# One matrix product from unsplit float32 blocks, behind dummy products, in a hand-ordered three-stage kernel

## The chip, the cores and the metric

The kernel runs on one core of one Trainium2 chip. The metric is device time in microseconds (us) of one execution. A difference of 0.2% or less can't be told from no change.

## What is computed

The reference chains three layers on two batches (b) of 768 positions and 512 channels.

```python
# attention: 8 heads of 64 channels, local window and block summaries
k_sum, v_sum = max and mean of k and v over blocks of 32      # 24 summaries
scores = concat(scale * q k^T where |i-j| < 16, scale * q k_sum^T + log 32)
x = softmax(scores) @ concat(v, v_sum)
# gated layer
gate = sigmoid(causal 5-tap convolution of x, per channel)
x = (gate * (x @ w_val)) @ w_out
# spatial gating
h = relu(x @ w_in);  u, v = halves of h
v_n = (v - mean(v)) / sqrt(var(v) + 1e-6)
out = (u * (w_spatial @ v_n + b_spatial)) @ w_out2
```

There is no nonlinearity between `w_out` and `w_in`, so the kernel forms the product `w_out @ w_in` once ("the weights' product"): 512x512 by 512x1024, and uses it in place of the two.

## The kernel before, in words

**Split products.** Large matrix products are made from a float32 operand split into a high and a low part in the format fp32r: `hi` is the rounded copy (ScalarE, CAST), `lo` is the difference (GpSimd, a tensor_tensor). A product is then three fp32r matmuls (hi·hi, hi·lo, lo·hi), `mm3` and `product`. Scores, transposes, the product with v and the means' matmuls use plain float32 operands.

**Loading weights.** The weights come as float64. `load64` loads a block of 128 rows by 512 numbers (512 KB) and turns it into float32: one ScalarE activation (Prelu) into PSUM, one VectorE tensor_scalar and one VectorE scalar_tensor_tensor. `split64` then makes `hi` and `lo` of it. `w_out` has 4 blocks, each half of `w_in` has 4 (threads `in0`, `in1`), `w_val` 4 and `w_out2` 4.

**The weights' product** (`w_product`) has two halves of 512 columns. For half 1 four PSUM banks collect over the four blocks, in four steps of 4x3 matmuls 128x128 by 512 columns. For half 0 (`OUTER = 1`) each of four steps makes one bank's 4x3 matmuls. ScalarE scales each result into a `wide` tile, which is split again later (`weights_v`, `weights_u`).

**Means of v.** `reduce_v` adds up the rows of v in a tree on VectorE. `put_vsum`, the first time for a batch, brings the 4x24 sums to partitions 96 to 119 by four float32 matmuls with a shifted identity (`moves`), and ScalarE scales them by 1/32 out of PSUM. GpSimd then copies them beside each pair's v (24x1536), which the product with v (`pv`) needs.

**Order.** The work is cut into pieces of named threads (`score`, `at`, `pv`, `wp`, ...). `ORDER` lists the pieces; the place in the list is the priority. `Planner.plan` simulates the engines with a table of costs and gives each engine, and the DMA queue on SP, a fixed order: at each point the operation that can start first, and of those within `LOOK` the one with priority. A PSUM tile may only be taken if it is among the first tiles not yet taken, as many as banks are free (8). SP keeps at most 8 transfers under way.

**SBUF.** 33 units of 128x1536 float32. A small tile is a part of a unit (`Parts`); the parts are dealt out as the program is recorded, and a unit comes free when all its parts are done with.

In the profile all instructions carry line 226, where the planner issues them; the tiles in SBUF units are all called at_u and those in PSUM at_ps.

Of the kernel before, what the change touches and what calls it, by code (L numbers as in the profile page):

```python
# [16 lines left out]
P = 128  # L17
# [19 lines left out]

SEVEN = {'val': (), 'u': (), 'v': ()}
# [4 lines left out]
    wout wval in0 in1 lk wout wp in1 wout lk kw wp wval kw in1 lk in0 lq wp wout lk mask lq in1 in0 kw lq*2 mask lv  # L43
    score wp in0 vsum score kw vsum lk wp score cw lv*2 lq put*2 score*2 wval at put lv put wp*2 lk at wval pv at
    score*2 wp pv at score lv lq at pv*2 gate val0 lk pv val0 at lv val0 at val0 lk wu at lv kw wu score wu pv kw wu
    wv at lq kw pv*2 score wv kw wv u0 vsum u0 gate wv score val0 vsum val0 u0 lv put*2 score*2 pv at lq val0 u0
    score*2 pv score at v0 put v0 put val0 at*3 pv*4 at pv at pv ws v0*2 gate val1 f0 val1 gate v0*2 val1*3 u1 val1
    out2 val1 ws s0 v1 u1 val1 v1*2 u1 f1 s1 f0 u1 ws v1*3 f1 s0 s1 f0 f1 u0 u1 s1*2 ws u1 s0*2 ws f1 u0 u1 u0 u1
    out2 f0 s0 out2 s0 u0 s1 s0*2 f0 s0 s1 out2 s0 ws f0*2 s0 s1 ws s1 s0 r s0*2 f1 r s1*2 r f1 s1 r*3 f1 s1*2 r*3
    s1 r*3  # L50
# [12 lines left out]
class Planner:  # L63
# [6 lines left out]
    def __init__(self, nc):  # L70
        self.ops, self.hist, self.tiles, self.cap = [], {}, {}, {}
        self.seq = 0
        self.piece, self.needs = [("start", 0)], {}
        self.homes, self.place = {}, {}
# [3 lines left out]
    def tile(self, ap, tag, bufs):  # L78

        name = ap.tensor.name if hasattr(ap, "tensor") else ap.name  # L80
        self.tiles[name] = [tag, None, 0]
        self.cap[tag] = bufs
        return ap
# [126 lines left out]
    def issue(self):  # L210
        order, real_ = self.plan(), {}

        def home(x):

            if not hasattr(x, "ap") or x.tensor.name not in self.place:
                return x
            name = x.tensor.name
            if name not in real_:
                tag, i = self.place[name]
                real_[name] = self.homes[tag](i, x.tensor)  # L220
            y = bass.AP(real_[name].tensor, x.offset, list(x.ap))
            return y if y.dtype == x.dtype else y.bitcast(x.dtype)

        for o in order:
            real, method, args, kw = o.call
            getattr(real, method)(*[home(x) for x in args], **{k: home(x) for k, x in kw.items()})  # L226

    def plan(self):
# [17 lines left out]
        held = {}  # L246
        open_, best, stale = {e: [] for e in free}, {e: None for e in free}, set(free)
# [8 lines left out]
        def slot_time(o):  # L256
            want = {}
            for n in o.tiles:
                if n in user:
                    want.setdefault(self.tiles[n][0], []).append(n)  # L260
            t = 0.0
            for tag, names in want.items():
                have = slots[tag]
# [33 lines left out]
        while len(order) < len(ops):  # L297
# [9 lines left out]
            if o.want:  # L307
                for n in sorted(o.tiles):
                    if n in user:
                        tag = self.tiles[n][0]  # L310
                        line[tag].remove(n)
                        held[n] = min(slots[tag])[1]
                        slots[tag].remove(min(slots[tag]))
                        if tag in self.homes:
                            self.place[n] = tag, held[n]
# [33 lines left out]
            for n in o.tiles:  # L349
                uses[n] -= 1  # L350
                if not uses[n]:
                    slots[self.tiles[n][0]].append((done + lat, held[n]))
                    stale.update(free)
# [7 lines left out]
        return order  # L361

# [10 lines left out]
def tile_kernel(ctx, tc, q, k, v, vn, w_val, conv_w, w_out, w_in, w_sp, b_sp, w_out2, mask_l, mask_r, eye, out):  # L373
# [19 lines left out]
    plan.homes["u"] = lambda i, x: homes.tile([P, 1536], x.dtype, tag=f"h{i}", name="at_" + x.name, bufs=1)  # L393

    def unit(dt=F32R):
        uid[0] += 1
        x = homes.tile([P, 1536], dt, tag="h0", name=f"u{uid[0]}", bufs=1)
        return plan.tile(x, "u", NU)

    class Parts:  # L400


        def __init__(self, n, dt=F32R):
            self.n, self.dt, self.free = n, dt, []

        def get(self):
            if not self.free:
                u = unit(self.dt)
                self.free = [u[:, self.n * i : self.n * (i + 1)] for i in reversed(range(1536 // self.n))]
            return self.free.pop()  # L410
# [45 lines left out]
    def load_masks():  # L456

# [15 lines left out]
        pool.memset(moves, 0.0)  # L473
        pool.affine_select(out=moves, in_=moves, pattern=[[-1, 264]], compare_op=ALU.not_equal, fill=1.0, base=112, channel_multiplier=1)
        yield

    def load64(src, n=512, queue=None):

        u = unit(F32)
        raw, t = u[:, : 2 * n], u[:, 2 * n : 3 * n]  # L480
# [12 lines left out]
    W = {}  # L493

    def split64(name, src, c):
        third = Parts(512)
        for i in range(KT):
            t = load64(src[i * P : (i + 1) * P, 1024 * c : 1024 * (c + 1)])
# [4 lines left out]
            yield  # L503

# [56 lines left out]
    def reduce_v(m):  # L561
# [13 lines left out]
        dve.tensor_add(MS[b][:, m % 2 * D : (m % 2 + 1) * D], t[:, :D], t[:, D : 2 * D])  # L575

    def put_vsum(n):
# [4 lines left out]
        need("mask", 2)  # L582
# [12 lines left out]
    def scores(t):  # L595
        n, g = ticks[t]
        need("mask", 1)
# [29 lines left out]
    def a_T(t):  # L627
        need("score", t + 1)
        need("mask", 2)
# [478 lines left out]

    def w_product():
# [5 lines left out]
        for n in (1, 0):  # L1115
            if n < OUTER:
                for e in range(KT):
                    po = psum()
                    for i in range(KT):
                        need("wout", i + 1)  # L1120
                        need(f"in{n}", i + 1)
                        mm3(po, [t[:, e * P : (e + 1) * P] for t in W["ot", i, 0]], W["in", i, n], i == 0, i == KT - 1)
# [4 lines left out]
            for i in range(KT):  # L1127
                need("wout", i + 1)
                need(f"in{n}", i + 1)
                for k, (a, b) in enumerate(((0, 0), (0, 1), (1, 0))):  # L1130
# [12 lines left out]
    def each(n, piece):  # L1143
# [6 lines left out]
        "lk": each(NPR, load_k), "lq": each(NPR, load_q), "mask": load_masks(), "kw": each(NPR, windows), "lv": each(NPR, load_v),  # L1150
# [3 lines left out]
        "wp": w_product(), "wv": each(KT, weights_v), "wu": each(KT, weights_u), "vs": each(2, weights_x), "us": each(2, weights_s), "nw": each(2, weights_n),  # L1154
# [120 lines left out]
```

## Time and profile before

| | |
|---|---|
| median of 3 runs | 271.32 us (271.19 to 271.7) |
| profiled execution, its own time | 271.58 us |
| its span, first to last instruction | 269.8 us |
| TensorE busy | 250.0 us, from 13.44 to 266.8 us |
| mean granted clock | 0.994 |

The profiled execution spends 1.78 us outside its span, and lies 0.26 us above the median. "Busy" counts the time from the start of an instruction to its end; the ends of matmuls are modelled. PE is TensorE, PEld its weight loads, DVE VectorE, ACT ScalarE, POOL GpSimd, SP the engine whose queue issues the loads.

### The profile page before, as it was taken

To read this page: it belongs to the slowest core of one execution; us is meant where nothing else is said; L and a number is where in the kernel's file an instruction comes from. 1 tells how busy PE (TensorE), PEld (TensorE's weight loads), DVE (VectorE), ACT (ScalarE), POOL (GpSimd) and SP (SyncE) were. 2 spreads that over 40 slices of the span, in tenths; PEclk is the share of its full clock that TensorE was granted. 3 is DMA by queue.
4 is the path that set the end of the run, shared out by engine and by line. 5 is a ranking of instruction groups with operands and counts; after the bars stand their busy time and mean duration, and the time that the engine had idled before them with its cause. 6 is when DMAs were issued, how large, how long until landed. Compare 5 with 4: busy or idle time off the path is not lost.

```text
span 269.8 us, 5493 instructions
## 1 busy us (share of the span) xinstructions
PE 250.0 (93%) x1912; PEld 224.8 (83%) x1912; DVE 190.0 (70%) x558; ACT 166.0 (62%) x452; POOL 180.4 (67%) x209
## 2 busy tenths in 40 slices
PE   0097999999999998999999999999999999999995
PEld 0075777868999996988899989899999999989885
DVE  3598888889989998899975969597452924572110
ACT  4687898899999999797353054512465755132221
POOL 7698864797898984993067167652869798883210
PEclk9999899999999999999999999999999999999999
DMA  6999998981452410460000010000003202022213
GB/s 208 405 406 406 312 359 271 325 297 35 137 167 61 117 32 1 129 226 1 2 1 0 10 70 0 0 2 0 0 4 137 97 0 80 0 78 78 80 39 117
DMA packets 11003, 31.63 MB, mean 117 GB/s; under 512 B 1552, under 2 KB 1824, under 8 KB 10976
## 3 DMA queue, kind: packets, MB, share of 16 engines
q1 hardware_dynamic: 10944, 31.27, 33.1%
q8 instruction: 15, 0.25, 0.4%
q14 instruction: 12, 0.10, 0.1%
q0 software_dynamic: 32, 0.02, 0.0%
HBM read 28.14 MB, written 3.15 MB: 116 GB/s over the span
## 4 chain that ended last, share of the span: by engine, by line
PE 79%; DMA 7%; DVE 5%; ACT 4%; SPq 2%; POOL 1%; issue 1%; DVEq 0%; ACTq 0%
PE at_ps L226 79%; DVE at_u L226 4%; DMA at_u<-in_k_dram 4%; ACT at_u L226 4%; DMA at_u<-in_moe_w_val_dram 2%; SPq L226 2%; DMA at_u<-in_v_dram 1%; POOL at_u L226 1%; DVE km L226 0%; ACT at_ps L226 0%; DVE nm L226 0%; DVE sm L226 0%; ACT xl L226 0%; DVEq L226 0%; ACTq L226 0%
## 5 line engine op out<-in xcount | busy, mean ns | idle before, releaser
L226 PE MATMUL at_ps<-at_u,at_u 128*128 128x384 f32 (+4 forms) x1800 | 239.1, 321 | 15.5 <-ACT at_u L226 15.5
L226 PEld LDWEIGHTS at_ps<-at_u,at_u 128*128 128x128 f32 (+2 forms) x1800 | 212.7, 188 | 38.7 <-ACT at_u L226 16.6
L226 POOL TENSOR_TENSOR at_u<-at_u,at_u 128x384 fp32r<-128x384 f32 (+2 forms) x95 | 116.9, 1251 | 48.9 <-ACT at_u L226 47.7
L226 ACT CAST at_u<-at_u 128x384 fp32r<-128x384 f32 (+2 forms) x95 | 53.4, 597 | 29.2 <-DVE at_u L226 19.8
L226 ACT COPY at_u<-at_ps 120x384 f32<-120x384 f32 (+3 forms) x61 | 28.4, 504 | 47.2 <-PE at_ps L226 47.2
L226 DVE TENSOR_TENSOR at_u<-at_ps,at_u 128x384 f32<-128x384 f32 (+1 forms) x36 | 19.7, 553 | 35.2 <-PE at_ps L226 33.8
L226 ACT ACTIVATE at_u<-at_u,nm 128x120 f32<-128x120 f32 x96 | 37.1, 401 | 1.6 <-DVE nm L226 1.6
L226 DVE SCALAR_TENSOR_TENSOR at_u<-at_ps,cw,at_u 128x384 f32<-128x384 f32 (+3 forms) x64 | 37.0, 608 | 0.2
L226 POOL TENSOR_TENSOR at_u<-at_u,sm 128x360 f32<-128x360 f32 x32 | 27.5, 882 | 13.3 <-DVE sm L226 11.2
L226 DVE CUSTOM_DVE_ANT_0 at_u<-at_ps,mask 128x120 f32<-128x120 f32 x96 | 21.6, 276 | 4.4 <-PE at_ps L226 4.3
L226 DVE TENSOR_SCALAR at_u<-at_u 128x512 uint32<-128x512 uint32 (+1 forms) x21 | 15.3, 731 | 6.8 <-DMA at_u<-in_moe_w_out_dram 5.3
L226 ACT ACTIVATION_READ_ACCUMULATOR at_u<-at_u,nm 128x1 f32 x96 | 19.7, 205 | 0.0
L226 ACT ACTIVATE at_ps<-at_u 128x512 f32<-128x512 f32 x20 | 12.9, 643 | 10.7 <-DMA at_u<-in_moe_w_out_dram 6.9
L226 POOL COPY at_u<-at_u 128x320 f32<-128x320 f32 (+2 forms) x24 | 17.8, 756 | 0.8 <-ACT at_u L226 0.2
L226 POOL TENSOR_TENSOR va<-va,power 128x1 f32<-128x1 f32 x12 | 7.4, 618 | 14.9 <-DVE va L226 8.8
L226 DVE TENSOR_TENSOR at_u<-at_u 128x384 f32<-128x384 f32 (+5 forms) x31 | 15.9, 515 | 0.1
L226 ACT ACTIVATE at_u<-at_ps 128x512 f32<-128x512 f32 (+1 forms) x22 | 12.6, 593 | 5.0 <-PE at_ps L226 4.9
L226 DVE TENSOR_TENSOR at_u<-at_u,at_u 128x256 f32<-128x256 f32 (+2 forms) x25 | 15.5, 628 | 0.1
L226 DVE SCALAR_TENSOR_TENSOR at_u<-at_ps,at_u 128x512 uint32<-128x512 uint32 x20 | 13.7, 689 | 2.1 <-ACT at_ps L226 0.8
L226 PE MATMUL at_ps<-moves,at_u 128*120 128x128 f32 x96 | 13.8, 276 | 0.4 <-POOL at_u L226 0.4
L226 DVE SCALAR_TENSOR_TENSOR at_u<-at_u,at_u 128x384 f32<-128x384 f32 x16 | 14.0, 905 | 0.1
L226 PEld LDWEIGHTS at_ps<-moves,at_u 128*120 128x120 f32 x96 | 10.9, 137 | 1.8 <-POOL at_u L226 0.6
(36 smaller groups left out, 116.4 us busy)
## 6 DMA issues: line engine op xcount, KB each, us to landing
at_u<-in_moe_w_out_dram SPq DMA_DIRECT2D x8, 512.0 KB, 5.0
at_u<-in_moe_w_in_dram SPq DMA_DIRECT2D x8, 512.0 KB, 9.0
at_u<-in_k_dram SPq DMA_DIRECT2D x8, 384.0 KB, 8.5
at_u<-in_q_dram SPq DMA_DIRECT2D x8, 384.0 KB, 8.1
at_u<-in_v_dram SPq DMA_DIRECT2D x16, 192.0 KB, 6.0
at_u<-in_vn_dram SPq DMA_DIRECT2D x6, 512.0 KB, 8.5
out_dram<-at_u SPq DMA_DIRECT2D x11, 256.0 KB, 2.0
at_u<-in_moe_w_spatial_dram SPq DMA_DIRECT2D x6, 384.0 KB, 5.8
```

Source lines behind the costliest of these rows:

```text
L226: getattr(real, method)(*[home(x) for x in args], **{k: home(x) for k, x in kw.items()})
```

## The change

1. `WHOLE = {0: 4, 1: 4}`: for all four blocks of both halves, the weights' product takes the unsplit float32 blocks, 32 float32 matmuls of 128x128 by 512 columns in place of 96 fp32r ones. The 12 blocks of `w_out` and `w_in` are no longer split; each lies in a `wide` tile. (`split_late` has no pieces with these values.)
2. A new thread `hot` of nine pieces (`awake`): each multiplies `moves` (128x264) by its first 128 columns into a PSUM tile that nobody reads. `load_masks` makes `moves` first, and the masks after it.
3. The means of v: ScalarE scales the sums (96x128) in place, and four DMAs from the SP queue move them, 24x128 each, to partitions 96 to 119. The four matmuls and the scaling out of PSUM are gone.
4. The planner places parts of units itself (`Units`): a part is taken when its first operation is planned and comes free on its own; parts of one kind share a unit.
5. `ORDER` is another list. `mask`, `in1`, `hot` and `wout` come first, the first four `wp` pieces are spread among the loads and the first scores, and the first `gate` stands again behind eight `score` and four `pv` pieces.

```diff
+WHOLE = {0: 4, 1: 4}
...
-    wout wval in0 in1 lk wout wp in1 wout lk kw wp wval kw in1 lk in0 lq wp wout lk mask lq in1 in0 kw lq*2 mask lv
-    score wp in0 vsum score kw vsum lk wp score cw lv*2 lq put*2 score*2 wval at put lv put wp*2 lk at wval pv at
...
+    mask in1 hot mask hot wout*2 in1 hot*4 in1 wval wout in1 lk lq hot wval wout lk wp lk wp hot lk kw*2 in0*2 score
+    wp lq*2 in0 score kw vsum wp lq in0 vsum score kw score lv score wp*2 at put cw pv lv put score wp at pv lv
+    wval*2 put at score*2 wp lv*2 at lk put hot lk at vsum lv at*2 pv*2 kw gate lq lv lq kw wu lq pv*2 val0 wu
...
+            whole = i < WHOLE[max(c, name == "ot")] and name in ("ot", "in")
+            t = load64(src[i * P : (i + 1) * P, 1024 * c : 1024 * (c + 1)], to=wide.get() if whole else None)
+            if whole:
+                T[name, i, c] = t
+                yield
+                continue
...
+    def awake(i):
+        need("mask", 1)
+        pe.matmul(psum()[:, :264], moves[:, :P], moves, start=True, stop=True)
...
+        if m % 2:
+            act.mul(MS[b], MS[b], 1.0 / 32)
...
         if b not in MEAN:
-            po = psum()
+            MEAN[b] = stage.get()[WK:KW]
             for i in range(4):
-                pe.matmul(po[:KW, i * 2 * D : (i + 1) * 2 * D], moves[: 4 * NS, 16 + i * NS : 16 + i * NS + KW], MS[b], start=True, stop=True, skip_group_check=True)
-            MEAN[b] = stage.get()[WK:KW]
-            act.mul(MEAN[b], po[WK:KW], 1.0 / 32)
+                sp.dma_start(MEAN[b][:, i * 2 * D : (i + 1) * 2 * D], MS[b][i * NS : (i + 1) * NS])
...
+                        if i < WHOLE[n]:
+                            pe.matmul(po, T["ot", i, 0][:, e * P : (e + 1) * P], T["in", i, n], start=i == 0, stop=i == KT - 1)
+                            continue
...
+                if i < WHOLE[n]:
+                    for e in range(KT):
+                        pe.matmul(pos[e], T["ot", i, 0][:, e * P : (e + 1) * P], T["in", i, n], start=i == 0, stop=i == KT - 1)
...
+class Units:
+    def take(self, kind):
+        t, i, j = self.pick(kind)
+        if None not in self.free[i]:
+            self.kind[i], self.free[i] = kind, [t] * (self.WIDTH // kind[1])
+            self.count += 1
+            self.names[i] = self.count
+        self.free[i][j] = None
+        return i, j
+    def give(self, at, t):
+        self.free[at[0]][at[1]] = t
```

## Rows read from the trace of the kernel before

**Rows 1.** The page: span and busy time of each engine, with the count of instructions.

```profile
span 269.8 us, 5493 instructions
PE 250.0 (93%) x1912; PEld 224.8 (83%) x1912; DVE 190.0 (70%) x558; ACT 166.0 (62%) x452; POOL 180.4 (67%) x209
```

**Rows 2.** Busy us of each engine by stretch, granted clock, DMA share, GB/s.

```profile
core 0: us, PE busy (x) PEld busy (x) DVE busy (x) ACT busy (x) POOL busy (x), PEclk, DMA share, GB/s
0.00:13.44 13.44, 0.00 (x0) 0.00 (x0) 6.03 (x10) 7.54 (x12) 9.35 (x26) 1.00 0.83 306
13.44:19.00 5.56, 5.56 (x13) 4.36 (x14) 5.11 (x8) 4.58 (x8) 5.09 (x8) 1.00 1.03 407
22.86:24.21 1.35, 0.00 (x0) 0.00 (x0) 1.25 (x3) 0.99 (x3) 0.41 (x1) 1.00 1.04 410
25.95:29.30 3.35, 3.35 (x15) 2.46 (x13) 2.80 (x10) 2.88 (x12) 3.35 (x8) 0.50 1.06 345
29.30:61.12 31.82, 30.73 (x317) 24.08 (x315) 27.14 (x116) 28.37 (x105) 23.16 (x26) 1.00 0.93 308
72.78:104.23 31.45, 30.51 (x386) 28.15 (x385) 29.14 (x133) 31.36 (x118) 25.59 (x33) 1.00 0.30 93
104.23:266.80 162.57, 162.55 (x1025) 150.38 (x1025) 101.49 (x241) 74.13 (x157) 99.27 (x90) 1.00 0.13 47
266.80:269.80 3.00, 0.00 (x0) 0.00 (x0) 0.00 (x0) 0.37 (x1) 0.00 (x0) 1.00 0.20 69
0.00:72.78 72.78, 56.90 (x503) 46.25 (x504) 59.33 (x188) 60.14 (x179) 55.59 (x87) 0.98 0.82 288
```

**Rows 3.** Timeline of the start: start, duration, engine, operation.

```profile
1.51 0.40 POOL L226 TENSOR_SCALAR_AFFINE_SELECT moves<-moves 128x264 f32<-128x264 f32 x1
4.16 0.66 ACT L226 ACTIVATE at_ps<-at_u 128x512 f32<-128x512 f32 x1 [2.14 <-DMA at_u<-in_moe_w_out_dram]
4.16 0.43 DVE L226 TENSOR_SCALAR at_u<-at_u 128x512 uint32<-128x512 uint32 x1 [4.16 <-DMA at_u<-in_moe_w_out_dram]
6.18 0.69 DVE L226 SCALAR_TENSOR_TENSOR at_u<-at_ps,at_u 128x512 uint32<-128x512 uint32 x1 [0.24 <-ACT at_ps L226]
13.44 9.42 PE L226 MATMUL at_ps<-at_u,at_u 128*128 128x512 f32 x36 [13.44 <-ACT at_u L226]
```

**Rows 4.** TensorE by shape, 13 to 62 us: calls, busy us, mean ns, idle before.

```profile
L226 PE MATMUL at_ps<-at_u,at_u 128*128 128x512 f32 x96 | 28.8, 453 | 14.8 <-ACT at_u L226 14.8
```

**Rows 5.** The same view, 200 to 266.8 us.

```profile
L226 PE MATMUL at_ps<-at_u,at_u 128*128 128x512 f32 x132 | 31.8, 391 | 0.0
L226 PE MATMUL at_ps<-at_u,at_u 128*128 128x256 f32 x24 | 3.0, 283 | 0.0
```

**Rows 6.** Timeline of TensorE and its weight loads at 104 us.

```profile
104.23 1.10 PE L226 MATMUL at_ps<-at_u,moves 96*120 96x128 f32 x8 [0.95 <-DVE at_u L226]
104.20 0.94 PEld L226 LDWEIGHTS at_ps<-at_u,moves 96*120 96x120 f32 x8 [1.34 <-issue]
```

**Rows 7.** TensorE by shape, 13 to 29.3 us.

```profile
L226 PE MATMUL at_ps<-at_u,at_u 64*64 64x120 f32 x24 | 2.4, 334 | 0.0
```

**Rows 8.** All groups by shape: calls, busy us, mean ns, idle before.

```profile
L226 POOL TENSOR_TENSOR at_u<-at_u,at_u 128x512 fp32r<-128x512 f32 x28 | 36.3, 1299 | 8.5 <-ACT at_u L226 7.6 <-DMA at_u<-in_v_dram 0.8
L226 ACT CAST at_u<-at_u 128x512 fp32r<-128x512 f32 x28 | 17.5, 625 | 2.5 <-DVE at_u L226 2.5
L226 PE MATMUL at_ps<-at_u,at_u 64*64 64x120 f32 x384 | 19.0, 309 | 0.0
```

**Rows 9.** VectorE by shape, 0 to 61 us.

```profile
L226 DVE TENSOR_SCALAR at_u<-at_u 128x512 uint32<-128x512 uint32 x16 | 12.9, 813 | 5.7 <-DMA at_u<-in_moe_w_out_dram 4.2 <-DMA at_u<-in_moe_w_in_dram 1.5
```

**Rows 10.** ScalarE's timeline: the first gate.

```profile
72.78 1.53 ACT L226 ACTIVATE at_u<-at_u 128x1536 f32<-128x1536 f32 x1
```

**Rows 11.** DMA issues: queue, count, KB each, median us to landing.

```profile
at_u<-in_v_dram SPq DMA_DIRECT2D x16, 92.0 KB, 4.2
```

**Rows 12.** What SP's queue waited for: us, times, longest.

```profile
SPq L226 <- ACT at_u L226: 56.1, 14, 15.9
```

More of the change, by code (lines that the diff above doesn't have):

```diff
@@ L217, in home @@
             name = x.tensor.name
[L218 to L221, printed above, removed]
+            tag, i, at, key = self.place[name]
+            if key not in real_:
+                real_[key] = self.homes[tag](i, x.tensor)
+            y = bass.AP(real_[key].tensor, x.offset + at, list(x.ap))
             return y if y.dtype == x.dtype else y.bitcast(x.dtype)
@@ L262, in slot_time @@
             for tag, names in want.items():
+                if tag == "u":
+                    reach, left = space.room(), len(names)
+                    for n in line[tag]:
+                        if not reach(self.kind[n]):
+                            return None
+                        left -= n in names
+                        if not left:
+                            break
+                    t = max(t, max(space.pick(self.kind[n])[0] for n in names))
+                    continue
                 have = slots[tag]
@@ L351, in plan @@
                 if not uses[n]:
-                    slots[self.tiles[n][0]].append((done + lat, held[n]))
+                    if self.tiles[n][0] == "u":
+                        space.give(held[n], done + lat)
+                    else:
+                        slots[self.tiles[n][0]].append((done + lat, held[n]))
                     stale.update(free)
@@ L361, in plan, with __init__, room, reach @@
         return order
+class Units:
+    WIDTH = 1536
+    def __init__(self, n):
+        self.kind, self.free = [None] * n, [[0.0] for i in range(n)]
+        self.names, self.count = [0] * n, 0
+    def room(self):
+        whole = sum(None not in x for x in self.free)
+        parts = {}
+        for k, x in zip(self.kind, self.free):
+            if None in x:
+                parts[k] = parts.get(k, 0) + len(x) - x.count(None)
+        def reach(kind):
+            nonlocal whole
+            if parts.get(kind, 0):
+                parts[kind] -= 1
+            elif whole:
+                whole -= 1
+                parts[kind] = self.WIDTH // kind[1] - 1
+            else:
+                return False
+            return True
+        return reach
+    def pick(self, kind):
+        some = [(-x.count(None), i) for i, x in enumerate(self.free) if self.kind[i] == kind and None in x and x.count(None) < len(x)]
+        if some:
+            i = min(some)[1]
+            t, j = min((t, j) for j, t in enumerate(self.free[i]) if t is not None)
+            return t, i, j
+        t, i = min((max(x), i) for i, x in enumerate(self.free) if None not in x)
+        return t, i, 0
+    def take(self, kind):
[8 more added lines that the diff above has]
+        self.free[at[0]][at[1]] = t
 class Recorder:
@@ L393, in tile_kernel, with unit @@
     plan.homes["u"] = lambda i, x: homes.tile([P, 1536], x.dtype, tag=f"h{i}", name="at_" + x.name, bufs=1)
-    def unit(dt=F32R):
+    kinds = [0]
+    def unit(dt=F32R, n=1536, kind=0):
         uid[0] += 1
         x = homes.tile([P, 1536], dt, tag="h0", name=f"u{uid[0]}", bufs=1)
-        return plan.tile(x, "u", NU)
+        return plan.tile(x, "u", NU, (kind, n))[:, :n]
     class Parts:
         def __init__(self, n, dt=F32R):
-            self.n, self.dt, self.free = n, dt, []
+            kinds[0] += 1
+            self.n, self.dt, self.kind = n, dt, kinds[0]
         def get(self):
[L407 to L410, printed above, removed]
+            return unit(self.dt, self.n, self.kind)
     def f(ap):
@@ L491, in load64 @@
         return t
-    W = {}
+    W, T = {}, {}
     def split64(name, src, c):
@@ L596, in scores @@
         n, g = ticks[t]
-        need("mask", 1)
+        need("mask", 2)
         need("lq", n + 1)
@@ L628, in a_T @@
         need("score", t + 1)
-        need("mask", 2)
+        need("mask", 1)
         for h in range(2):
@@ L1107, in weights_u, with split_late @@
         W["p", e, 0] = halves(W32.pop((0, e)))
+    def split_late(i):
+        need("wout", i + 1)
+        if i >= WHOLE[0]:
+            W["ot", i, 0] = halves(T["ot", i, 0])
     def w_product():
```

52 lines of the change are left out of this document (31 added, 21 removed).

## The prediction

> **What bounds the kernel now.** I read the page first: TensorE is busy for 250.0 of 269.8 us, no other engine for more than 190 [rows 1]. Then the busy time by stretch, to see where TensorE is not busy [rows 2]. It starts at 13.44, stands still from 22.86 to 24.21 (1.35 us), for 31.82 - 30.73 = 1.09 between 29.30 and 61.12, for 31.45 - 30.51 = 0.94 between 72.78 and 104.23, and then has no idle time until 266.80; 3.0 us follow for the last result. So the span is 13.44 + 250.0 + 3.4 of gaps + 3.0. A change counts if it moves the start, the sum of TensorE's work, or a gap. Third, the start in the timeline [rows 3]: the first block is there at 4.16, the second is float32 at 6.18 + 0.69 = 6.87, yet the first matmul waits for ScalarE and GpSimd, which split the blocks, until 13.44.
>
> The clock counts too. From 13.44 to 19.00, 13 matmuls of 512 columns take 5.56 us, 428 ns each, which is 512 columns at 1.2 GHz; the column for the granted clock reads 1.00 there, and I go by the durations. (The Trainium skill, "TensorE: Matmul & The Clock Gate", Seeing it yourself, warns that the clock records can be unreliable; by the record there would be no slow start to save.) After the stop at 22.86 the record does fall, to 0.50 from 25.95 to 29.30 [rows 2].
>
> VectorE is the second bound: until 72.78 it is busy 59.33 us [rows 2]. A TensorE that runs ahead will meet it.
>
> **The change part by part.**
>
> *The weights' product.* Before, its 96 matmuls cost 28.8 us [rows 4]; at the full clock such a matmul takes 31.8 / 132 = 0.241 us [rows 5]. After, there are 32 plain float32 matmuls of the same size, which the trace does not show. The nearest rows are the means' matmuls: four of 128 columns are eight records, in 1.10 us [rows 6], so one product is two records of 137 ns. The line through fp32r matmuls of 256 columns (3.0 / 24 = 125 ns) and of 512 (241 ns) is 9 ns + 0.453 ns a column [rows 5]; at twice the slope a record of 128 columns comes to 125 ns, near the 137. With that slope, 512 columns take 2 x (9 + 0.906 x 512) = 946 ns, and 32 of them 30.3 us: 1.5 more than before. Bounds: two records at the fp32r pace, 32 x 2 x 0.241 = 15.4, and all 1.10 / 4 growing with the columns, 32 x 1.10 = 35.2. I take 30.3, since the 137 ns speak against the lower end and include fixed time.
>
> A rule of the Trainium skill speaks against this edit: "FP8 and Floating Point Precision", TensorE Precision Notes, gives true float32 four passes through the array, against the three fp32r matmuls. By it the product would be 32 x 4 x 0.241 = 30.8, the term 2.0 in place of 1.5. The 137 ns for two passes of 128 columns agree.
>
> *Start and dummies.* `moves` was ready at 1.51 + 0.40 = 1.91 behind part of the masks [rows 3]; made first, I put it at 1.7. A dummy of 264 columns costs 264 / 128 x 0.275 = 0.57 at the full clock, 1.13 at half. Before, the clock took from 13.44 to 19.00, 5.56 us, to rise. So five dummies run slowly to 7.3 and the next ones fast. Two of the nine stand in the list behind PSUM tiles of the first `wp` pieces and run late; seven end at about 8.4. The data of the first product is there at 6.9, on the old landings. I take a start at 8.2: -5.2. Bounds: 6.9 (-6.5), and all nine first, 9.5 (-3.9). The late two add 2 x 0.55 = 1.1.
>
> *Scores at the low clock.* The 24 score records up to 29.3 us cost 2.4 [rows 7], the mean of all 384 is 19.0 / 384 = 0.049 [rows 8]: 24 x 0.049 = 1.2, so -1.2 if the clock stays up. Bounds -1.2 and 0.
>
> *The splits.* Twelve CASTs of 0.625 us on ScalarE (7.5) and twelve differences of 1.30 on GpSimd (15.6) go [rows 8]. They are off the path except at the start, already counted. They also lay beside VectorE: its tensor_scalar on a block takes 0.43 alone [rows 3] and 0.81 on average up to 61 us [rows 9]. For 12 blocks that is up to 12 x 0.38 = 4.6 us of VectorE.
>
> *The feed.* What is late next is the first gate, at 72.78 [rows 10]. By then TensorE had worked 56.90 [rows 2]; after the change 56.9 + 1.5 - 1.2 - 1.1 (a mean's matmuls) = 56.1, so it would get there at 8.2 + 56.1 = 64.3. VectorE, at 59.3 - 4.6 of work and the same 13.4 of idle time, gets there at 68.2. So TensorE must find some 4 us of other work or stop. The new list has other products ready (half 0 from 23 us on, the later scores), and the parts of SBUF that come free singly let loads start earlier, so I put all gaps at 3.0, against 3.4: -0.4. Bounds: none (-3.4) and 9 (+5.6).
>
> *The means.* Their eight matmuls go, twice 1.10: -2.2 [rows 6]. The gap of 0.95 before the second set, which waited for VectorE, is among the gaps. In their place ScalarE's scaling and four transfers: about 0.3 us, and some 4 until they land (a transfer of 92 KB takes 4.2 [rows 11]; four of 12 KB should need no more), against 1.10 and 0.59 for the scaling. The copies on GpSimd and `pv` of the batch start 2.6 us later. Scores and products cover that; if they didn't, TensorE would lose 2.6 a batch, within the gaps' bound. On SP the transfers wait for ScalarE, and the loads of k, q and v behind them wait too; SP's queue waited 56.1 us for ScalarE before without starving TensorE [rows 12].
>
> *The placing of parts* issues no instruction of its own. Reuse is finer, so a load may wait for another part than before; the gaps' bounds hold it.
>
> The sum: -5.2 + 1.5 + 1.1 - 1.2 - 0.4 - 2.2 = -6.4. The span goes from 269.8 to 263.4, the execution, with its 1.78 outside the span, to 265.2. The profiled execution lay 0.26 above the median, so the median comes to **264.9** against 271.32.
>
> **The rivals.**
>
> *TensorE is fed throughout.* No gaps after the start, and the product at the array's pace: the gaps give 3.0 more and the product perhaps 1: 260.9. For it: the gaps were only 2.0 after 24.21. Against: VectorE's 68.2 above.
>
> *VectorE keeps its pace.* GpSimd, rid of the splits, does its other work in the same places, tensor_scalars stay slow, and the first gate stays at 72.78. Then only what comes behind it is saved: 1.10 of means and 0.94 of gap, less a late dummy of 0.57: 271.32 - 1.5 = 269.8. For it: VectorE is busy 27.14 of 31.82 and 29.14 of 31.45 around it [rows 2]. Against: 13.4 us of idle time before the gate, half of it in the first 13.44 us.
>
> *No change.* The weight loads of plain float32 are not hidden behind a matmul. The means' loads took 0.94 for eight, 0.117 each [rows 6]; 64 of them uncovered cost 7.5, which turns 264.9 into 272.4, and with 55 uncovered the change does nothing (271.3). Against: in those rows 0.94 of loads lie inside 1.10 of matmuls.
>
> *Slower.* TensorE runs ahead and stops again and again between 23 and 64 us, and the clock falls after each stop. The stop of 1.35 us was followed by 3.35 at half rate [rows 2], together 1.35 + 1.68 = 3.0 lost. The sum holds 3.0 of gaps. So from the point where stops cost 9.4 the gain is gone, a little over three of this size; four give 264.9 + 12.1 - 3.0 = 274.0. For it: the load-bound stretch, DMA share 0.93 and more [rows 2]. Against: there was one such stop in all.
>
> **How the numbers follow.** Forecast 0.60 (262.5 to 267.5), fed throughout 0.13, VectorE's pace 0.11, no change 0.05, slower 0.11. So faster by over 0.2% (what a measurement here can tell) 0.60 + 0.13 + 0.11 = 0.84, within it 0.05, slower 0.11. The range has to take in the second and third case, with the product's and the start's bounds: 260.0 to 270.0.
>
> **What would show it.** Right: in the timeline TensorE's dummies from about 1.7 and its first 512-column product at 7 to 9; 64 records of 512 columns in about 30 us; no CAST and no difference of 128x512 in the first 25 us; tensor_scalars nearer 0.43; the first gate between 64 and 69; no gap at the second means. Wrong: products over 1.05 us each, gaps of TensorE over 6 us between 20 and 70 or a granted clock of 0.5 there more than once, a gate still at 72, or a TensorE that waits for `pv`'s v behind the means' transfers.

## The result, and the profile after

The changed kernel takes 269.01 us (median of four runs, 268.58 to 269.44) against 271.51 for the kernel before beside it: 0.9904 of it, 95% interval 0.9876 to 0.9932. It is faster, as forecast, but by 2.5 us where 6.4 were forecast. The rows are of an execution of 269.44 us.

The page, first the span, then the busy time of each engine; it answers to [rows 1]:

```profile
span 267.7 us, 5433 instructions
PE 255.7 (96%) x1882; PEld 220.7 (82%) x1882; DVE 189.3 (71%) x558; ACT 158.1 (59%) x440; POOL 164.1 (61%) x197
```

Busy us by stretch, as in [rows 2]:

```profile
0.00:8.25 8.25, 5.46 (x15) 4.06 (x15) 2.39 (x5) 2.83 (x4) 4.44 (x21) 1.00 0.74 245
8.25:30.00 21.75, 20.68 (x132) 11.19 (x133) 17.66 (x57) 15.89 (x38) 9.69 (x23) 1.00 1.03 406
30.00:45.00 15.00, 14.42 (x85) 7.71 (x84) 14.21 (x70) 13.67 (x64) 7.25 (x11) 1.00 0.93 280
45.00:60.00 15.00, 11.10 (x129) 7.64 (x128) 8.82 (x33) 11.78 (x42) 9.67 (x11) 1.00 0.77 248
...
60.00:65.00 5.00, 5.00 (x102) 4.76 (x100) 4.96 (x14) 4.75 (x13) 2.02 (x2) 0.66 1.06 247
...
8.25:264.65 256.40, 250.23 (x1868) 216.64 (x1868) 186.94 (x554) 154.89 (x436) 159.64 (x176) 0.99 0.34 115
```

TensorE's timeline to 75 us, those of its rows that begin behind a stop (the bracket: how long it stood, and what ended that); it answers to the start in [rows 3]:

```profile
8.25 1.95 PE L230 MATMUL at_ps<-at_u 128*128 128x512 f32 x4 [0.92 <-DVE at_u L230]
11.28 1.12 PE L230 MATMUL at_ps<-at_u,at_u 128*128 128x512 f32 x2 [1.07 <-DVE at_u L230]
32.77 3.98 PE L230 MATMUL at_ps<-at_u,at_u 64*64 64x120 f32 x30 [0.58 <-DMA at_u<-in_q_dram]
47.09 1.88 PE L230 MATMUL at_ps<-at_u,at_u 64*64 64x120 f32 x44 [0.90 <-ACT at_u L230]
49.61 3.70 PE L230 MATMUL at_ps<-at_u,at_u 128*128 128x512 f32 x8 [0.63 <-ACT at_u L230]
53.50 0.99 PE L230 MATMUL at_ps<-at_u,at_u 120*64 120x64 f32 x24 [0.19 <-POOL at_u L230]
59.28 1.20 PE L230 MATMUL at_ps<-moves,at_u 128*120 128x128 f32 x9 [2.18 <-DVE at_u L230]
```

The account that the prediction opened for the kernel before closes here as 8.25 of start + 250.23 of work + 6.17 of stops (256.40 - 250.23) + 3.05 behind the last product = 267.7. Against before: start -5.2, work +0.2, stops +2.8, end the same: -2.1. Nearly all the stops lie ahead of 59.28 us; from 45 to 60 TensorE works 11.10 of 15 us. From 60 to 65 the granted clock is 0.66. From 8.25 to 30 us the DMA engines are busy throughout (share 1.03, 406 GB/s), as they were from 13.44 us before the change [rows 2]; from 45 to 60, where TensorE stands most, their share is 0.77. So the start came at the forecast's figure, and over half of it was given back within 51 us.

What holds TensorE there is told by ScalarE's timeline and by the chain of waits that ends at 59.28 (start, us, what):

```profile
45.90 0.63 ACT L230 ACTIVATE at_ps<-at_u 128x512 f32<-128x512 f32 x1 [1.56 <-DMA at_u<-in_moe_w_val_dram]
```

```profile
39.82 1.99 ACT at_u L230 x7
41.80 6.63 DMA at_u<-in_moe_w_val_dram
48.44 0.02 issue
48.45 0.77 SPq L230
...
52.70 4.15 DMA at_u<-in_k_dram
56.85 0.02 issue
56.88 0.96 DVE km L230
...
59.24 0.04 issue
59.28 0.76 PE at_ps L230 x5
```

A load of `w_val` lands late, and ScalarE stands 1.56 us in front of its conversion; TensorE's stop of 0.90 before 47.09 is ended by ScalarE. On SP's queue the rest comes later still: the means' transfers, then k of the second batch, which TensorE needs through VectorE. SP's own timeline, one row for a run of transfers of one kind, which includes waits inside the run:

```profile
26.89 14.18 SPq L230 DMA_DIRECT2D at_u<-in_v_dram  x12
41.17 1.81 SPq L230 DMA_DIRECT2D at_u<-in_moe_w_val_dram  x2
43.03 3.70 SPq L230 DMA_DIRECT2D at_u<-in_v_dram  x6
46.82 3.91 SPq L230 DMA_DIRECT2D at_u<-at_u  x4
50.84 1.19 SPq L230 DMA_DIRECT2D at_u<-in_v_dram  x2
52.07 1.05 SPq L230 DMA_DIRECT2D at_u<-in_k_dram  x2
```

The four transfers of the means, 12 KB each, take 3.91 us of the queue. The second goes out at 48.45, when a load of `w_val` that was issued at 41.80 has landed (41.80 + 6.63 = 48.43): this program issues a transfer only when the one eight places ahead of it has landed, whatever their sizes.

### The profile page after: what moved, and what is told of

The parts are those of the page before. It is cut to its first block, busy times and chain, and to the rows that moved or that the text cites. A ratio compares the mean times of both kernels' runs of the same rounds, so it can differ in the third digit from the quotient of the medians.

```text
span 267.7 us, 5433 instructions
## 1 busy us (share of the span) xinstructions
PE 255.7 (96%) x1882; PEld 220.7 (82%) x1882; DVE 189.3 (71%) x558; ACT 158.1 (59%) x440; POOL 164.1 (61%) x197
## 2 busy tenths in 40 slices
DMA packets 11291, 31.73 MB, mean 119 GB/s; under 512 B 1648, under 2 KB 2112, under 8 KB 11264
## 4 chain that ended last, share of the span: by engine, by line
PE 73%; DMA 17%; SPq 3%; POOL 3%; ACT 2%; DVE 1%; issue 1%; DVEq 0%; ACTq 0%
PE at_ps L230 73%; DMA at_u<-in_moe_w_out_dram 6%; DMA at_u<-in_k_dram 5%; DMA at_u<-in_q_dram 4%; SPq L230 3%; POOL at_u L230 3%; DMA at_u<-in_moe_w_val_dram 2%; ACT at_u L230 2%; DVE at_u L230 0%; DVE km L230 0%; ACT at_ps L230 0%; DVEq L230 0%; ACTq L230 0%
## 5 line engine op out<-in xcount | busy, mean ns | idle before, releaser
L230 PE MATMUL at_ps<-at_u,at_u 128*128 128x384 f32 (+4 forms) x1752 | 233.5, 323 | 4.0 <-ACT at_u L230 2.1
L230 PEld LDWEIGHTS at_ps<-at_u,at_u 128*128 128x128 f32 (+2 forms) x1752 | 202.4, 190 | 31.6 <-issue 11.6
L230 POOL TENSOR_TENSOR at_u<-at_u,at_u 128x384 fp32r<-128x384 f32 (+2 forms) x83 | 102.8, 1261 | 53.1 <-ACT at_u L230 50.9
L230 ACT CAST at_u<-at_u 128x384 fp32r<-128x384 f32 (+2 forms) x83 | 45.3, 589 | 32.1 <-DVE at_u L230 26.7
L230 POOL TENSOR_TENSOR at_u<-at_u,sm 128x360 f32<-128x360 f32 x32 | 25.1, 814 | 18.9 <-ACT at_u L230 9.5
L230 DVE SCALAR_TENSOR_TENSOR at_u<-at_ps,cw,at_u 128x384 f32<-128x384 f32 (+4 forms) x64 | 36.3, 610 | 0.0
L230 ACT ACTIVATE at_ps<-at_u 128x512 f32<-128x512 f32 x20 | 13.0, 652 | 20.7 <-DMA at_u<-in_moe_w_out_dram 11.4
L230 DVE TENSOR_TENSOR at_u<-at_u,at_u 128x256 f32<-128x256 f32 (+2 forms) x25 | 19.8, 793 | 1.3 <-PE at_ps L230 0.7
L230 ACT ACTIVATE at_u<-at_ps 128x512 f32<-128x512 f32 x20 | 11.6, 596 | 14.2 <-PE at_ps L230 14.1
L230 DVE TENSOR_SCALAR at_u<-at_u 128x512 uint32<-128x512 uint32 (+1 forms) x21 | 11.5, 547 | 9.3 <-DMA at_u<-in_moe_w_in_dram 5.6
L230 DVE BATCH_NORM_STATS2 st<-at_u 128x6 f32<-128x512 f32 x12 | 8.2, 688 | 7.3 <-ACT at_u L230 7.3
```

## Experiments

Times vary by chip, so each kernel is given as its ratio to the kernel before on the same chip, with the 95% interval; 0.001 is 0.27 us, and the changed kernel stands at 0.9904. "Plan kept" means that the order is that of the changed kernel, and the edit sits in `issue`, where the planned operations are handed out (line numbers in the rows shift with it). The theories named in the expectations: S, the start and the unsplit product are worth what they were priced at; F, engines that work in order stand in front of single late loads, so the order of the loads matters; V, VectorE's work sets the pace; L, the transfers bind as a sum, eight under way at most, so that a load moved ahead makes another late.

**Without dummies.**

```diff
+            if o.piece[0] == "hot":
+                continue
```

> The changed kernel with its planned order kept, less the nine dummy products. Theory S (the start is worth what it was priced at): the first product still starts near 8.2 us, but at 1.2 GHz for some 5.6 us, which loses 2.8 us; the time goes from 269.0 to 271 or more. Theory F (TensorE waits for loads that SP's queue issues late, 6 us of gaps between 10 and 60 us): most of the 2.8 us goes into waiting that is there anyway; the time stays within 268.5 to 270. Theory V (VectorE's work sets the pace until the first gate at 71.2): the gate moves by less than 0.5 us and so does the end.

0.9892 (0.9853 to 0.993): the same as with them. Its first products run at half the rate:

```profile
8.14 3.78 PE L232 MATMUL at_ps<-at_u 128*128 128x512 f32 x4 [8.14 <-DVE at_u L232]
...
45.00:60.00 15.00, 11.56 (x129) 8.21 (x128) 8.79 (x35) 12.71 (x44) 10.82 (x12) 0.92 0.79 240
```

Four records take 3.78 us where 1.95 were needed behind the dummies. But they fill the stop of 1.07 at 10.2, so the third pair of records is only 1.1 us behind (13.35 for 12.24), and the late dummies' 1.3 us are saved. The dummies are worth nothing here. S had said 271 or more and is in doubt, but 1.1 us is too little to settle what an early start is worth; the late start below does that.

**The means' transfers from ScalarE's queue, and GpSimd's zeroing of v's tiles early; then both.** The zeroing (`memset`) is put as early as its tile is free.

```diff
+            if method == "dma_start" and o.piece[0] == "put":
+                real = self.ACT.real
...
+            if o.call[1] == "memset" and o.piece[0] == "lv":
+                done.insert(i, o)
```

> The changed kernel with its planned order kept; only the eight transfers of the means are issued from ScalarE's queue in place of SP's. Theory F: SP no longer spends 3.9 us on the first four, the loads of k for batch 1 are issued near 48 us in place of 52.1, the copies of the means on GpSimd start near 46 to 48 in place of 52.0, VectorE's wait of 4.3 us for k shrinks, and the time falls to 265.5 to 267.5. Theory V: the loads move, but the first gate stays within 0.5 us of 71.2 and the time at 268.5 to 269.5. Theory S says nothing changes, since neither the start nor the product does.

> The changed kernel with its planned order kept, but GpSimd's zeroing of each v tile, for which SP's loads of v wait, is put as early on GpSimd's queue as its SBUF unit allows. Theory F: SP is released sooner between 30 and 46 us, the loads behind come 0.5 to 3 us earlier, time 267 to 268.5. Theory V: first gate and time unchanged within 0.5 us. If the 8 transfers under way are what holds SP, and not GpSimd, nothing changes either.

> Both edits of the two runs before: means from ScalarE's queue and early zeroing. Theory F: the effects add, time 264.5 to 267, first gate at 66 to 69. Theory V: time 268.5 to 269.5, first gate within 0.5 us of 71.2.

ScalarE's queue: 1.0006 (0.9987 to 1.0025), the whole gain lost. Early zeroing: 0.9883 (0.9847 to 0.992), no difference that can be told. Both: 1.0003 (0.9978 to 1.0028). The first shows TensorE at 6.61 us of work from 40 to 50 in place of 8.47, and ScalarE here:

```profile
48.20 0.66 ACT L232 ACTIVATE at_ps<-at_u 128x512 f32<-128x512 f32 x1 [4.43 <-DMA at_u<-in_moe_w_val_dram]
...
44.97 0.82 SPq L232 DMA_DIRECT2D at_u<-in_moe_w_val_dram  x2
```

The loads of `w_val` left SP at 44.97 in place of 41.17, and ScalarE stood 4.43 us. So freeing SP of the means this way made the loads later, not earlier; neither F nor V had this. The chain of waits shows why SP fell behind (start, us, what):

```profile
42.67 2.23 DMA at_u<-at_u
...
44.97 3.21 DMA at_u<-in_moe_w_val_dram
...
48.21 3.86 DMA at_u<-at_u
```

ScalarE, behind its other work, issues the first transfer of the means at 42.67; it lands at 44.90, and only then does SP issue the load of `w_val`, for which ScalarE then stands until 48.20 before it can issue the next transfer of the means. In this program the eight places are one count over both queues: the means left SP's queue, but kept their places, and SP stood 3.2 us for one of them. So the run is no test of F.

**k of the second batch ahead of v's third pair,** without and with early zeroing.

```diff
+            if o.piece[0] == "lk" and o.piece[1] in (4, 5) and o.call[1] == "dma_start":
+                done.insert(i, o)      # i: behind v's second pair on SP's queue
```

> The changed kernel with its planned order kept on every engine; only the two loads of k for batch 1 that SP issues at 52.1 us, behind the means' transfers, are put ahead of the loads of v's third pair, near 33 us. Theory F (late loads stop the in-order engines, and TensorE behind them): VectorE's wait of 4.3 us at 50.8 goes, TensorE's gap of 2.2 us at 57 goes with it and the clock stays up after it, time 265.5 to 267.5. Theory L (the transfers are bound by their sum: what is loaded earlier pushes the v and w_val loads back by 2 us): gaps move to 45 to 55 us, time 268.5 to 270.

> The edit of the run before together with the early zeroing of v's tiles. Theory F: 265 to 267. Theory L: 268 to 270.

0.9903 (0.9867 to 0.9939) and 0.9885 (0.9857 to 0.9913): no gain. In the first the stop of 2.18 us in front of the transposes is gone, and another has come:

```profile
49.08 7.91 PE L230 MATMUL at_ps<-at_u,at_u 64*64 64x120 f32 x76 [2.73 <-ACT at_u L230]
```

That speaks for L: k came earlier, `w_val` later (at 42.02 on SP in place of 41.17).

**The means by matmuls again, and the product from split blocks again;** both planned anew with the new list (in the second `WHOLE = {0: 0, 1: 0}`).

```diff
-                sp.dma_start(MEAN[b][:, i * 2 * D : (i + 1) * 2 * D], MS[b][i * NS : (i + 1) * NS])
+                pe.matmul(po[:KW, i * 2 * D : (i + 1) * 2 * D], moves[: 4 * NS, 16 + i * NS : 16 + i * NS + KW], MS[b], start=True, stop=True, skip_group_check=True)
...
-WHOLE = {0: 4, 1: 4}
+WHOLE = {0: 0, 1: 0}
```

> The changed kernel with the means moved by matmuls again as before the change; the planner makes a new order from the same list. TensorE gets 2.2 us of work back. Theory F (the transfers of the means lie in SP's way and land late): put starts 5 us earlier and TensorE's gaps between 45 and 60 us shrink by more than 2.2, time at or below 269. Theory L: gaps as they are, time 270.5 to 272.

> The changed kernel with the weights' product from split blocks again (96 fp32r matmuls, 12 CASTs and 12 differences back), dummies, means, parts and list as changed; the planner makes a new order. TensorE's work falls by 30.6 - 23 to 28, that is 3 to 7 us, ScalarE gets 7.5 and GpSimd 15.6 us back. If the unsplit product is what the change gains by: first product near 12 us, more gaps, time 271 to 276. If the gain is in the list and the start alone: 266 to 270.

1.0046 (1.0 to 1.0092) and 1.0471 (1.0428 to 1.0513). The split product starts nearly as early and then stops again and again, for ScalarE and GpSimd:

```profile
8.83 0.50 PE L230 MATMUL at_ps<-at_u,at_u 128*128 128x512 f32 x1 [0.80 <-ACT at_u L230]
9.65 0.49 PE L230 MATMUL at_ps<-at_u,at_u 128*128 128x512 f32 x1 [0.32 <-POOL at_u L230]
10.88 6.88 PE L230 MATMUL at_ps<-at_u,at_u 128*128 128x512 f32 x22 [0.74 <-POOL at_u L230]
```

The first is at or above the upper end of what L had said, the second beyond both expectations. The list was not made for these two, so they don't price the parts; they show that the new list is no gain without the parts that it was made for.

**What does the work on SP's queue cost?** First the means' transfers left out; second v's two large transfers of a pair issued as one.

```diff
+            if o.piece[0] == "put" and method == "dma_start":
+                continue
...
+            if o.piece[0] == "lv" and method == "dma_start" and args[0].ap[0][1] == 64:
+                d, s = args
+                if d.offset % 1536:
+                    continue
+                args = [bass.AP(x.tensor, x.offset, [list(x.ap[0]), [1, 1536]]) for x in args]
```

> Plan kept; the eight transfers of the means are left out, and GpSimd's copies read a constant instead of the means of v, so the block means do not enter the product. ScalarE still scales the sums. Theory L (the transfers, eight under way at most, are late as a whole): SP is free of 3.9 us of issuing and of four places among the eight, the loads of k for the second batch are issued at about 48 instead of 52.07, TensorE's stop of 2.18 us before 59.28 shrinks below 1, idle time of TensorE between 45 and 60 falls from 3.9 to 2 or less, time 267. Theory V (VectorE's work sets the pace): the date of the first gate and the time stay within 0.5 us of 269.0.

> Plan kept; the two large transfers of each pair's v, 64 partitions each, are issued as one of twice the bytes, so 32 transfers of v become 24. Theory L, if the count of transfers under way matters: v's first three pairs are issued 1.5 to 3 us sooner, what follows them on SP's queue too (the load that TensorE waits for before 47 us, the means', k), idle time between 45 and 60 falls below 3, time 267.5 or less. L, if only the bytes matter: no change, 269.0 within 0.5. V: no change either.

0.9794 (0.9769 to 0.9819) and 0.9844 (0.9817 to 0.987): 3.0 and 1.6 us less than the changed kernel. Without the means' transfers (SP, TensorE from 45 to 60, the first gate):

```profile
49.74 0.96 SPq L240 DMA_DIRECT2D at_u<-in_k_dram  x2
...
45.00:60.00 15.00, 13.16 (x156) 9.11 (x155) 9.78 (x36) 12.66 (x44) 10.34 (x12) 0.89 0.95 277
...
68.58 1.50 ACT L240 ACTIVATE at_u<-at_u 128x1536 f32<-128x1536 f32 x1
```

Merged v (SP):

```profile
27.03 12.34 SPq L235 DMA_DIRECT2D at_u<-in_v_dram  x9
```

Without the means' transfers k leaves SP at 49.74 in place of 52.07, TensorE stands 1.84 us of the 15 shown in place of 3.90, and the first gate comes at 68.58 (before: [rows 10]; after: 71.19). VectorE's work is the same (189.2 us against 189.3), so V falls. The run also frees GpSimd's copies from waiting for the means, so it does not tell the place on the queue from the lateness of the means. Merging v moves no byte less, and SP's run of v's first three pairs shrinks from 14.18 to 12.34 us: fewer, larger transfers of the same bytes get through sooner. Whether it is the count of transfers or the size of their packets (10651 in place of 11291 in all), the run does not tell. The Trainium skill, "SBUF — State Buffer", The DMA setup-cost knee, says that each transfer pays a part that does not grow with its bytes, and asks for the largest single transfers; here the traces agree: with the means on ScalarE's queue 12 KB took 2.23 and 3.86 us to land, and v's 192 KB took 4.5 in the median.

**The list and the placing of parts,** each put back to that of the kernel before, planned anew.

```diff
-    mask in1 hot mask hot wout*2 in1 hot*4 in1 wval wout in1 lk lq hot wval wout lk wp lk wp hot lk kw*2 in0*2 score
+    mask hot*7 wout wval in0 in1 lk wout wp in1 wout lk kw wp wval kw in1 lk in0 lq wp wout lk mask lq in1 in0 kw lq*2 mask lv
...
-            return unit(self.dt, self.n, self.kind)
+            if not self.free:
+                u = unit(self.dt)
+                self.free = [u[:, self.n * i : self.n * (i + 1)] for i in reversed(range(1536 // self.n))]
+            return self.free.pop()
```

> All of the change but its list: the list of the kernel before, with the first mask piece and seven dummies put in front (the other two dummies fall to the end of the list), planned anew. If the new list is what makes the loads late (more of v's and w_val's early), the gaps of TensorE after its start come back to 3.4 to 4.5, and the time is 265 to 267. If the start is simply absorbed because the loads' sum, not their order, sets the date by which TensorE is fed, the first gate again comes at 70 to 73 and the time is 268 to 272.

> All of the change but the placing of parts: parts are dealt out of whole units as the program is recorded, as in the kernel before, and the plan is made anew with the new list. If the finer placing lets loads start sooner, loads come later here and the time is 1 to 4 us longer (270 to 273). If it is neutral: 269.0 within 0.8. If its finer reuse is what makes loads wait for a neighbour, the gaps between 45 and 60 shrink and the time is 266 to 268.

The old list: 1.0301 (1.0264 to 1.0338). With it the first product starts at 13.88 us all the same, 6.24 us after the dummies, released by VectorE: the two blocks that it needs first are the first and the fourth that the old list loads. Neither expectation was met; the new list is a necessary part of the early start. The old placing: 0.9888 (0.9865 to 0.991), no difference.

**All that helped together.** Left out means' transfers, merged v, early zeroing; then the last two alone, with the whole computation; then these with k ahead of the means on SP's queue; and merged v in the kernel before.

```diff
+            if o.piece[0] == "lk" and o.piece[1] in (4, 5) and o.call[1] == "dma_start":
+                done.insert(i, o)      # i: ahead of the means' transfers on SP's queue
```

> Plan kept; three edits together: v's large transfers issued as one per pair, GpSimd's zeroing of v's tiles early, and the means' eight transfers left out (GpSimd's copies read a constant, so the block means do not enter the product). Theory L, and the three are separate costs on SP's queue: their single gains add up, about 3.0 + 1.6 + 0.6 = 5.2 us, time 264, first gate near 66, and nearly the whole of the forecast comes back. L, but all three relieve one and the same wait: no more than the means' transfers alone, 266 to 267. A limit behind the loads (VectorE, ScalarE): 266 or more, with TensorE's remaining stops released by these engines while SP's queue is ahead.

> Plan kept, whole computation: v's large transfers issued as one per pair, and the zeroing of v's tiles early. L with separate costs: 269.0 - 1.6 - 0.6, about 266.8, faster than the changed kernel. L with one wait: 267.5, as with the merged transfers alone.

> As the run with merged transfers and early zeroing, and on SP's queue the two loads of k for the second batch are issued ahead of the four transfers of the means. If what the means' transfers cost is the delay of k behind them (some 4 us on SP's queue), TensorE's stop before its transposes at 57 to 59 us goes and the time falls by another 1 to 2 us, to 265.5. If they cost through the places they hold among the eight under way, or the means are now late for the product with v, no gain: 266.8 or more, with a stop of TensorE released by GpSimd in its place.

> The kernel before, plan kept, with v's large transfers issued as one per pair. If transfers bound the front only since the change (before, TensorE's gaps between 29 and 61 us were 1.09), no more than 0.5 us: 271.0. If they bound it before as well, the same 1.6 us as in the changed kernel: 269.8.

0.978 (0.9735 to 0.9824), 0.9806 (0.9771 to 0.984), 0.9802 (0.9765 to 0.9838) and 1.0021 (0.9996 to 1.0045). The three do not add up: on top of the other two, leaving out the means' transfers gives 0.0026, inside the intervals, where alone it gave 0.0110. That they relieve one and the same wait is the nearest reading; that engines behind the loads set the rest is not excluded. Merged v with early zeroing keeps the whole computation and is faster than both kernels, 267.55 us beside 272.0 in the median (the quotient of these medians, 0.984, is the upper end of the interval). What the early zeroing adds to merged v (0.9844) is within the intervals. The execution in the trace, at 266.08 us the fastest of six, has fewer and shorter stops:

```profile
47.38 6.67 PE L235 MATMUL at_ps<-at_u,at_u 64*64 64x120 f32 x76 [0.83 <-ACT at_u L235]
57.52 1.20 PE L235 MATMUL at_ps<-moves,at_u 128*120 128x128 f32 x9 [0.84 <-DVE at_u L235]
```

With k ahead of the means the stop at 57 goes, and GpSimd's copies, whose means now come later, make one of 2.37 (GpSimd itself stands 2.35 for them):

```profile
55.22 0.92 PE L235 MATMUL at_ps<-at_u,at_u 120*64 120x64 f32 x24 [2.37 <-POOL at_u L235]
```

In the kernel before, merged transfers gain nothing. That its TensorE started late enough not to wait for them fits its gaps (1.09 us from 29 to 61), but its list and its means are others too, and no run separates these.

**The start put back, and `w_val` ahead of v.** In the first, each of the seven dummies at the start is issued three times. The second is the merged version with early zeroing, with the two loads of `w_val` ahead of v's third pair.

```diff
+            if o.piece[0] == "hot" and o.piece[1] < 7:
+                for again in range(2):
+                    getattr(real, method)(*[home(x) for x in args], **{k: home(x) for k, x in kw.items()})
...
+            if o.piece[0] == "wval" and o.call[1] == "dma_start":
+                done.insert(i, o)      # i: behind v's second pair on SP's queue
```

> Plan kept; each of the seven first dummies is issued three times, so that TensorE's first product starts at about 13.5 us, as in the kernel before, in place of 8.25. The forecast's premise, that the start reaches the end in full: the stop of 1.07 at 10.2 goes, the rest of the delay stays, 269.0 + 5.2 - 1.1 = 273.1. Theory L (the date by which TensorE is fed after 45 us is set by the loads, and the early start only waits for them later): the stops before 60 us shrink by most of the delay, the first gate stays within 1 us of 71.19, time 269.0 to 270.5.

> Plan kept, whole computation: v's large transfers merged, zeroing early, and the two loads of w_val at 40 us issued ahead of v's third pair. F (ScalarE stands in front of the conversion of w_val, 1.56 us at 44.3 in the changed kernel, and what TensorE needs is queued behind it): the stop before 47 us goes, time 266 (0.977 of before). L (the transfers bind as a sum): the third pair of v comes that much later, GpSimd and the product with v wait in place of ScalarE, no gain over the run with merged transfers and early zeroing alone (0.981 of before); more, if SP's queue stands still at the moved loads because their place in SBUF isn't free yet (0.985 or more).

The late start: 0.987 (0.9841 to 0.9898), 267.99 us beside 271.61; 273.1 was the premise's figure. This is the decisive run. The first product starts at 13.98, k leaves SP at 51.50 against 52.07, and TensorE:

```profile
13.98 1.88 PE L233 MATMUL at_ps<-at_u 128*128 128x512 f32 x4
...
51.50 1.05 SPq L233 DMA_DIRECT2D at_u<-in_k_dram  x2
...
59.05 1.20 PE L233 MATMUL at_ps<-moves,at_u 128*120 128x128 f32 x9 [0.68 <-DVE at_u L233]
63.01 2.24 PE L233 MATMUL at_ps<-at_u,at_u 120*64 120x64 f32 x27 [0.40 <-issue]
...
1.87:58.37 56.50, 56.40 (x377) 35.16 (x377) 40.94 (x158) 41.18 (x143) 29.33 (x56) 1.00 0.91 325
13.98:262.65 248.67, 247.48 (x1869) 214.83 (x1867) 185.55 (x547) 151.52 (x432) 160.31 (x176) 1.00 0.32 109
```

From 1.87 to 58.37 it does not stop (0.10 us idle in all); then 0.68 and 0.40, nearly all its stops behind the first product. A start 5.7 us later costs nothing, because the transposes begin at 59.05 in place of 59.28: they wait, through VectorE, for k, which leaves SP at nearly the same time. That date does not depend on the start. That the loads alone set it is argued: the chain ahead of k runs through a load of `w_val` in the changed kernel and through GpSimd (until 50.54) in this run. The account: 13.98 + 247.5 of work + 1.2 of stops (248.67 - 247.48) + 3.05 = 265.7 us of span. The run does a little better than L had said (269.0 or more): the first gate comes at 70.11, 1.08 ahead of 71.19.

`w_val` ahead: 0.9857 (0.983 to 0.9885), no gain over 0.9806, and the last of the expectation's branches: SP's run of the two loads takes 2.74 us in place of 1.04. The stop for ScalarE shrinks to 0.51, and TensorE has one of 2.44 for GpSimd in its place, which itself stands 2.44 for the means' transfers:

```profile
53.71 1.55 PE L235 MATMUL at_ps<-at_u,at_u 120*64 120x64 f32 x24 [2.44 <-POOL at_u L235]
```

Three times, then, a load moved ahead removed its stop and made another elsewhere. So each single stop is F's, a late load; and in these three runs their sum behaved as L says.

## Why the prediction was off

The step that failed is *the feed*: "TensorE must find some 4 us of other work or stop", and "I put all gaps at 3.0". It stops for 6.2, so the term is +2.8 in place of -0.4: 3.2 of the 4.3 us by which the span, 267.7, lies above the forecast's 263.4. Most of the rest is work, +0.2 in place of -0.8. The step asked when VectorE would reach the first gate (68.2); what the runs showed in its place is the date of a load: TensorE's transposes wait for k of the second batch until 59.28, and until 59.05 with a start 5.7 us later. So the stops took back over half of the start's -5.2 and slow matmuls behind them another part, and the run with the late start shows that nothing is left of it. Point by point:

- Start: forecast 8.2, measured 8.25, and that close by luck. The seven dummies end at 7.33 (by the prediction's own terms they would have ended at 1.7 + 5 x 1.13 + 2 x 0.57 = 8.5, later than the start that it took), and the blocks were not there at 6.9: VectorE ends a stop of 0.92 ahead of the first product, and the second step stands another 1.07. Without dummies the first product starts at 8.14.
- Product: forecast 30.3. The 340 records of 512 columns take 97.1 us, less 66.4 for the 276 of them after 60 us: 30.7 for 64 records, 0.96 a product. The slope from the small matmuls was good. The Trainium skill, "FP8 and Floating Point Precision", TensorE Precision Notes, led to 30.8: the trace agrees. This counts each record to its modelled end; from start to start a product takes 0.86 us here (pairs of records begin at 12.24, 13.10 and 13.96).
- Late dummies: 18 records take 6.8 us, 5.46 of them at the start: 1.3, forecast 1.1.
- Scores: 17.7 against 19.0 [rows 8], -1.3, forecast -1.2. But the product with v takes 14.1 us where it took 12.7, after the stops, with the clock at 0.66 from 60 to 65; the run with the late start has 12.7 again (both rows stand below the list). In that run the work behind the start, the same matmuls, is 247.5 us, 2.7 less than in the changed kernel: 1.4 of it here and 0.6 in the scores (17.1). That these are slow matmuls behind the stops fits the granted clock, 1.000 over that run and 0.994 here. The rows by shape overlap, so the 1.0 by which work missed the forecast can't be split among its terms.
- Means: the eight matmuls are gone, and the gap at 104 us too. "Four of 12 KB should need no more" priced how long they fly, not the 3.91 us of SP's queue, which the sum put at nothing. The argument from [rows 12], that SP could wait without starving TensorE, was taken from a TensorE that starts at 13.44.
- Splits: VectorE's 20 tensor_scalars fall from 15.1 to 11.4 us, 3.7 where up to 4.6 were allowed. VectorE was named as what is late next; the runs showed the transfers in its place. The first gate came at 71.19, outside the 64 to 69. Of the prediction's signs of being wrong none showed clearly: products of 0.96 us, 4.5 us of gaps between 20 and 70 where it asked for over 6, one fall of the clock, a gate just short of 72, and 0.19 us of waiting in front of the product with v. The bound on the gaps was too wide to show a loss of 3.
- Rivals: 269.8, "VectorE keeps its pace", is near the number, for another reason. What happened is the mechanism of "Slower", a TensorE that runs ahead and stops again and again, at stops of 6.2 us in place of the 9.4 at which the gain would have been gone. The clock did fall after stops, once, from 60 to 65 us in this execution; two of the four runs kept the full clock and took 268.58 and 268.75, so the fall does not explain the missing 3.9 us.
- Where the gain does come from: against [rows 1, 2] the run with the late start begins 0.5 us later, has 2.5 us less work (the means alone are 2.2) and 2.2 us fewer stops.

The product with v, in the changed kernel and with the late start:

```profile
L230 PE MATMUL at_ps<-at_u,at_u 120*64 120x64 f32 x384 | 14.1, 239 | 0.2 <-POOL at_u L230 0.2
...
L233 PE MATMUL at_ps<-at_u,at_u 120*64 120x64 f32 x384 | 12.7, 224 | 0.4 <-issue 0.4
```

Still open: why the three edits together leave 2 us of stops between 45 and 60, whether the means' transfers cost by their place on the queue or by their lateness, and whether merged transfers with a late start would gain more; that was not run.

## What to carry to other kernels

In this kernel a start that was moved ahead was worth only what the next loads allowed: lay the dates at which later loads land beside the dates at which they will now be wanted, before you count it. The test is cheap: put the start back with dummy work and see whether the time notices. On a queue with a fixed number of transfers under way, count the transfers as well as the bytes, ask whether another queue's transfers take places in the same count, and when one load is moved ahead, name the one that is late in its stead.

## What was not expected of the hardware

- Four transfers from SBUF to SBUF of 12 KB held SP's queue for 3.91 us, a wait for a landing included, and 4.93 where they stood behind k's.
- Without dummies the column of the granted clock reads 1.00 from 8 to 12 us, while the first products there take twice their time (3.78 against 1.95 us for four records).
- Fewer, larger transfers of the same bytes gave 1.6 us in the kernel whose TensorE waited for them, and none in the kernel before (1.0021).
